# Work off PSUM traced in lagged steps, each placed behind its engine's instructions so far

## The chip, the cores and the metric

The kernel runs on one core of one Trainium2 chip. The metric is device microseconds of one execution; a time is the median of several runs. A core has a matrix engine (TensorE; PE in the profile, with its weight loads as PEld), VectorE (DVE), ScalarE (ACT), GpSimd (POOL) and DMA queues, most of which are fed here from the sync engine (SP). Each engine works off its own instructions in the order in which the program lists them, and waits at an instruction until the data and buffers that it needs are there.

## The reference

Eight batches of eight-head attention over 576 positions of width 64, with a causal mask, a bias of cumulated sums and a softmax; then a layer on the joined heads (512 channels): a two-dimensional Fourier transform of which the real part is kept, an addition, a normalisation, a two-layer net with a ReLU, and a residual.

```python
def _attn_ref(q, k, v, s):
    scores = scale * np.matmul(q, k.transpose(0, 1, 3, 2))        # (8, 8, 576, 576)
    cum = np.cumsum(np.maximum(s, 0.0), axis=-1)
    bias = -(cum[:, :, :, None] - cum[:, :, None, :])
    scores = np.where(causal, -1e9, scores + np.minimum(bias, 0.0))
    attn = np.exp(scores - np.max(scores, axis=-1, keepdims=True))
    attn = attn / (np.sum(attn, axis=-1, keepdims=True) + 1e-09)
    return np.matmul(attn, v)

def _moe_ref(x, w_ch1, w_ch2):                                    # x: (8, 576, 512)
    mixed = np.real(np.fft.fft(np.fft.fft(x, axis=1), axis=2))
    u = x + mixed
    un = (u - mean(u)) / np.sqrt(var(u) + 1e-06)                   # over the channels
    return u + np.maximum(un @ w_ch1, 0.0) @ w_ch2                 # 512 -> 2048 -> 512
```

## The kernel before, in words

To hold fp32 accuracy on TensorE, nearly every operand is split into a high part and the rest (`split`, L68 to L70: ACT copies the high part, DVE subtracts it), and a product is three passes: high by high, high by low, low by high.

**The attention loop.** 64 heads are worked in 32 pairs, `for i in range(NP)`, and an iteration holds pieces of several pairs: the score products whose row maxima are wanted for pair i+1 (`maxes`: a matmul into `pm`, L459, and a DVE reduction, L466; 12 of each), the high and low parts of the queries and keys (`high(i+2)`: ACT copies, L418 and L420; `low(i+1)`: the keys' rest `k` on DVE, L435, the queries' rest on POOL, L438), the scores and exponentials of pair i (`scores`: L491, L492 into `ps`, ACT's exponential L495), the product with the values of pair i-1 (`av`, into `pav`, moved out by ACT to `stage`, L527), and the division of pair i-2 (`recip` and `finish`: sums plus 1e-9 and a reciprocal on DVE, L538 and L539, out to memory and back as a broadcast `rb`, L544, then a product, L559, and its transfer into `xs`). `pm` and `pav` share five PSUM buffers; `ps` and the products of the Fourier stage share another pool of three.

Four pairs make a batch. When a batch is there, `folds` forms its symmetric and antisymmetric halves (`Aw`, `Bw`, `Df`, split into `De` and `Do`; L251 to L268) in iterations i with i % 4 == 2 (five of seven steps) and i % 4 == 3 (the rest), and `fourier` does the transforms in the iterations that follow: matmuls into `pzs` and `pzc`, split from PSUM into `zs` and `zc`, a second set into `pyc` and `pys`, sums `ym` and `yp` (L320, L321), and additions on POOL (L324 and on).

**The weights** come as 64-bit numbers in pieces of 256 columns, four for each of 16 blocks f of the net. `rounded` (L83 to L89) makes fp32 of one piece: exponent bits on DVE (L83), a scaled ReLU on ACT (L84), the mantissa on DVE (L85, L88), sign and exponent together on DVE (L87), a product on POOL (L89). In the attention loop `convert_w` writes the first blocks back to memory (L98). The remaining blocks are converted while the first token tile of the net runs (`load_w`): `rounded`, then the high part `wh` on ACT (L112) and the rest `wl`, on DVE for the first two pieces and on POOL for the last two (L114).

**The net** takes nine tiles of 512 tokens. Per block f: 12 matmuls into `h` (L183), which need the pieces 0 and 1 of `wh` and `wl`; `zh` on ACT (L187) and `zl` on DVE (L188); and 12 matmuls into four accumulators (L196 to L198), which need pieces 2 and 3.

**What sets the order.** TensorE's order is the order in which the program is traced (`manual_schedule`). The generators of an iteration are interleaved by `weave`, which at each turn advances the one that has used the smallest share of its own total; a `yield` returns a cost, and the second entry of each pair in the list is the total. The order of all other engines is made by a scheduler, from when an instruction was traced and from a model of when it could start; so an instruction there need not stand where it was traced.

## Time and profile before

| | |
|---|---|
| median of 3 runs | 1428.55 us (1426.3 to 1429.79) |
| the profiled execution's own time | 1426.1 us |
| its span in the profile | 1424.4 us |
| PE busy | 1305.1 us, 92% of the span, 6190 matmuls |
| DVE busy | 745.7 us, 52% |
| ACT busy | 539.3 us, 38% |
| POOL busy | 561.6 us, 39% |
| mean granted TensorE clock | 0.971 of full speed |

The page of the profile gives busy time by engine, the span in 40 slices of 35.6 us with the busy share of each in tenths, and groups of instructions by line. Other views give the engines' busy time in chosen windows, the waits with the instruction that ended each, and single instructions in order of time, with the idle time before one in brackets and what ended it. In a group's row the first number behind the bar is busy microseconds, the next mean nanoseconds of one, and behind the second bar stands the idle time ahead of them. The net's first tile starts some 600 us into the span, when the attention is done; from about 703 us on all weights are converted and eight tiles follow each other.

### The profile page before, as it was taken

How to read it: one execution, taken by the hardware profiler on the slowest of the kernel's cores; microseconds unless marked ns; L12 is line 12 of the kernel's file. 1: busy time of each engine (PE TensorE's matmuls, PEld its weight loads, DVE VectorE, ACT ScalarE, POOL GpSimd, SP SyncE). 2: the span in 40 equal slices, each digit the busy share in tenths (PEclk: the TensorE clock that was granted, in tenths of full speed). 3: DMA queues.
4: the chain of work that ended last, by engine and by line, in shares of the span. 5: the costliest groups of instructions: out<-in, count | busy, mean ns of one | idle time of the engine just before them, and what ended most of it. 6: DMA issues, size and time to landing. Idle time of an engine off the chain costs nothing.

```text
span 1424.4 us, 17997 instructions
## 1 busy us (share of the span) xinstructions
PE 1305.1 (92%) x6190; PEld 1068.7 (75%) x6190; DVE 745.7 (52%) x1684; ACT 539.3 (38%) x1211; POOL 561.6 (39%) x543
## 2 busy tenths in 40 slices
PE   4887979897988887997899999999999999999998
PEld 3766868686777676775688888888888888888886
DVE  6667677877777788799833233222332223322212
ACT  4775756676665656344321121211212112121110
POOL 6445465656546566565720402204022040123300
PEclk9998999999999997999899999999999999999999
DMA  8555556565655555433200000000000000000000
GB/s 214 156 159 144 163 149 180 158 168 159 159 161 144 166 149 163 162 123 121 79 8 30 31 30 15 15 30 31 30 15 15 30 30 30 15 16 0 30 0 30
DMA packets 78230, 125.05 MB, mean 88 GB/s; under 512 B 11256, under 2 KB 36249, under 8 KB 78139
## 3 DMA queue, kind: packets, MB, share of 16 engines
q1 hardware_dynamic: 75627, 119.83, 28.4%
q0 software_dynamic: 1696, 2.50, 0.9%
q10 hardware_dynamic: 816, 1.57, 0.3%
q8 instruction: 49, 0.80, 0.2%
q14 instruction: 42, 0.34, 0.1%
HBM read 76.85 MB, written 23.07 MB: 70 GB/s over the span
## 4 chain that ended last, share of the span: by engine, by line
PE 51%; DVE 7%; POOL 2%; DMA 1%; issue 1%; ACT 1%; SPq 0%; DVEq 0%; POOLq 0%; ACTq 0%
PE h L183 25%; PE acc L198 8%; PE acc L196 8%; PE acc L197 8%; POOL we L89 1%; DVE wm L88 1%; DVE we L83 1%; DVE wm L85 1%; DVE we L87 1%; DVE wl L114 1%; ACT wh L112 1%; DMA wl<-wD 0%; POOL wl L114 0%; DVE ucl L148 0%; DVE zl L188 0%
## 5 line engine op out<-in xcount | busy, mean ns | idle before, releaser
L188 DVE SCALAR_TENSOR_TENSOR zl<-h,zh 128x512 fp32r<-128x512 f32 x144 | 98.6, 686 | 405.5 <-ACT zh L187 405.4
L187 ACT ACTIVATE zh<-h 128x512 fp32r<-128x512 f32 x144 | 85.9, 596 | 530.1 <-PE h L183 530.1
L198 PE MATMUL acc<-zl,wh 128*128 128x512 f32 x576 | 227.5, 396 | 4.9 <-DVE zl L188 4.9
L196 PE MATMUL acc<-zh,wh 128*128 128x512 f32 x576 | 227.6, 395 | 1.0 <-ACT zh L187 1.0
L197 PE MATMUL acc<-zh,wl 128*128 128x512 f32 x576 | 226.8, 394 | 0.0
L523 PE MATMUL pavB<-P,va 128*128 128x320 f32 (+2 forms) x640 | 189.1, 389 | 9.5 <-ACT stage L527 8.9
L459 PE MATMUL pm<-KQ 128*128 128x256 f32 (+3 forms) x384 | 156.5, 427 | 44.4 <-DVE Mx L466 23.1
L495 ACT ACTIVATE P<-ps 128x320 f32<-128x320 f32 (+4 forms) x384 | 145.9, 393 | 110.5 <-PE ps L492 106.8
L491 PE MATMUL ps<-KQ 128*128 128x256 f32 (+2 forms) x384 | 154.1, 404 | 24.4 <-ACT P L495 14.0
L183 PE MATMUL h<-uch,wh 128*128 128x512 f32 x576 | 159.9, 398 | 8.3 <-ACT wh L112 8.3
L183 PE MATMUL h<-uch,wl 128*128 128x512 f32 x576 | 158.1, 396 | 0.8 <-DVE wl L114 0.8
L183 PE MATMUL h<-ucl,wh 128*128 128x512 f32 x576 | 156.9, 393 | 0.0
L466 DVE CUSTOM_DVE_ANT_0 trash<-pm,amask 128x128 bf16<-128x128 f32 (+3 forms) x256 | 123.5, 482 | 34.2 <-PE pm L459 16.9
L212 POOL TENSOR_TENSOR o<-o,w 128x512 f32<-128x512 f32 x32 | 41.8, 1305 | 252.3 <-issue 218.5
L183 PEld LDWEIGHTS h<-uch,wh 128*128 128x128 f32 x576 | 108.2, 190 | 35.9 <-ACT wh L112 12.1
L198 PEld LDWEIGHTS acc<-zl,wh 128*128 128x128 f32 x576 | 108.7, 189 | 32.0 <-DVE zl L188 6.9
L183 PEld LDWEIGHTS h<-uch,wl 128*128 128x128 f32 x576 | 109.2, 190 | 26.6 <-DVE wl L114 1.2
L196 PEld LDWEIGHTS acc<-zh,wh 128*128 128x128 f32 x576 | 108.6, 188 | 26.1 <-ACT zh L187 1.8
L183 PEld LDWEIGHTS h<-ucl,wh 128*128 128x128 f32 x576 | 108.9, 189 | 24.7
L197 PEld LDWEIGHTS acc<-zh,wl 128*128 128x128 f32 x576 | 108.6, 189 | 24.7
L459 PEld LDWEIGHTS pm<-KQ 128*128 128x128 f32 x384 | 78.4, 207 | 64.7 <-DVE Mx L466 30.2
L492 PE MATMUL ps<-q,k 128*128 128x256 f32 (+2 forms) x384 | 120.5, 316 | 3.1 <-POOL q L438 3.1
(140 smaller groups left out, 2066.9 us busy)
## 6 DMA issues: line engine op xcount, KB each, us to landing
qk<-in_qkT_dram SPq DMA_DIRECT2D x32, 576.0 KB
raw<-in_wP_dram SPq DMA_DIRECT2D x64, 256.0 KB
va<-in_vA_dram SPq DMA_DIRECT2D x32, 480.0 KB
q<-KQ SPq DMA_DIRECT2D x32, 288.0 KB
k<-KQ SPq DMA_DIRECT2D x32, 288.0 KB
rb<-rd SPq DMA_DIRECT2D x64, 144.0 KB
u<-uD SPq DMA_DIRECT2D x8, 1024.0 KB
out_dram<-o SPq DMA_DIRECT2D x32, 256.0 KB
```

The lines of the kernel that those rows point to most:

```text
L183: nc.tensor.matmul(h[:, :n], a[:, j * 128:(j + 1) * 128], b[:, j, :n], start=i == 0, stop=i == 11)
L187: nc.scalar.activation(zh[:, :n], h[:, :n], AF.Relu)
L188: nc.vector.scalar_tensor_tensor(out=zl[:, :n], in0=h[:, :n], scalar=0.0, in1=zh[:, :n].bitcast(F32), op0=ALU.max, op1=ALU.subtract)
L196: nc.tensor.matmul(acc[j][:, :n], a[:, cs], y[:, :n], start=g == 0, stop=False)
L197: nc.tensor.matmul(acc[j][:, :n], b[:, cs], y[:, :n], start=False, stop=False)
L198: nc.tensor.matmul(acc[j][:, :n], a[:, cs], z[:, :n], start=False, stop=g == NF - 1)
L459: nc.tensor.matmul(p[:, :n], qy[:, h, 128 * c:128 * c + 128], ky[:, h, k0:k0 + n], start=True, stop=True)
L466: nc.vector.tensor_tensor_reduce(out=trash[:nq, :n], in0=p[:nq, :n], in1=amask[:nq, m0:m0 + n], scale=1.0, scalar=first if x else NEG, op0 ...
L491: nc.tensor.matmul(p[:, :n], ky[:, h, ksl], qy[:, h, a:a + n], start=True, stop=False)
L492: nc.tensor.matmul(p[:, :n], k1[:, h, ksl], q1[:, h, a:a + n], start=False, stop=True)
L495: nc.scalar.activation(P[:, o:o + a + n - lo], p[:, lo - a:n], AF.Exp, scale=0.125)
L523: nc.tensor.matmul(p[:, a - lo:n], va[:, c, vs], P[:, o:o + w], start=c == 0, stop=c == cs[-1])
```

## The change

A new helper, `behind(engine)`, orders an instruction behind the last one that has been traced so far for that engine. It adds no wait on data. With it:

- `rounded` yields between its DVE, ACT and POOL steps. Its first and its last DVE operation, its ACT operation and its POOL product are each placed behind what their engines have so far; the mantissa pair stays free. The transfer in `convert_w` is placed behind SP's.
- `folds` makes each `Df`, its high part and its rest in three steps, the last two placed. Of a cost of 6.6 (7 before), 0.7 is worked off in iterations i % 4 == 2 and 0.3 in i % 4 == 3; before it was five sevenths and two sevenths.
- `fourier` places the rest of each split behind DVE's, half a step after the copy, and waits two more steps at its end before it writes out.
- The copies of `high`, the differences of `low` and the transfer of sums in `av` are placed. `low` and `high` start later in an iteration, and `low` at the same point in every iteration.
- `recip` and `finish` become one generator, `post`, in five steps, each placed.
- `weave` passes on the costs of what it interleaves, and `later` yields its delay in one piece.

```diff
+    def behind(engine):
+        return tc.issue_after(next(i for i in reversed(nc.cur_bb.bb.instructions) if i.engine == engine))
...
-        yield 0.0
+        yield 0.3
         e = pool.tile([128, WC], I32, tag="we", name="we", bufs=bufs)
-        nc.vector.tensor_scalar(e, hi, 0x7FF00000, None, op0=ALU.bitwise_and)
-        nc.scalar.activation(e, e, AF.Relu, bias=wbias, scale=8.0)
+        with behind(ET.DVE):
+            nc.vector.tensor_scalar(e, hi, 0x7FF00000, None, op0=ALU.bitwise_and)
+        yield 0.2
+        with behind(ET.Activation):
+            nc.scalar.activation(e, e, AF.Relu, bias=wbias, scale=8.0)
         nc.vector.tensor_scalar(m, hi, 0xFFFFF, 0x100000, op0=ALU.bitwise_and, op1=ALU.bitwise_or)
-        yield 0.4
-        nc.vector.scalar_tensor_tensor(out=e, in0=hi, scalar=-0x80000000, in1=e, ...)
         nc.vector.scalar_tensor_tensor(out=m.bitcast(F32), in0=lo, scalar=2.0 ** -16, in1=m, ...)
-        nc.gpsimd.tensor_mul(e.bitcast(F32), m.bitcast(F32), e.bitcast(F32))
-        yield 0.4
+        yield 0.2
+        with behind(ET.DVE):
+            nc.vector.scalar_tensor_tensor(out=e, in0=hi, scalar=-0x80000000, in1=e, ...)
+        yield 0.1
+        with behind(ET.Pool):
+            nc.gpsimd.tensor_mul(e.bitcast(F32), m.bitcast(F32), e.bitcast(F32))
+        yield 0.2
...
-            yield 1.0
-            d = fft.tile([128, 289], F32, tag="Df", name="Df")
-            nc.vector.tensor_add(d, a[:, 0:289], a[:, 576:287:-1])
-            split(De[0][:, jj], De[1][:, jj], d)
-            yield 1.0
...
+            yield 0.6
+            for D, n in ((De, 289), (Do, 288)):
+                d = fft.tile([128, 289], F32, tag="Df", name="Df")
...
+                yield 0.6
+                with behind(ET.Activation):
+                    nc.scalar.copy(D[0][:, jj], d[:, :n])
+                yield 0.6
+                with behind(ET.DVE):
+                    nc.vector.tensor_sub(D[1][:, jj], d[:, :n], D[0][:, jj].bitcast(F32))
+                yield 0.0
...
-            split(zs[0][:, c], zs[1][:, c], p[:96, 0:256])
-            yield 650
+            nc.scalar.copy(zs[0][:, c], p[:96, 0:256])
+            yield 325
+            with behind(ET.DVE):
+                nc.vector.tensor_sub(zs[1][:, c], p[:96, 0:256], zs[0][:, c].bitcast(F32))
+            yield 325
...
-            streams.append([later(low(i + 1), i % 4 == 0), (6, 7, 4, 3)[i % 4]])
+            streams.append([later(low(i + 1), 1.5), 7.5])
...
-            streams.append([high(i + 2), 6])
+            streams.append([later(high(i + 2), 2), 6.5])
...
-            streams.append([later(call(recip, i - 2), 4), 10])
-            streams.append([later(call(finish, i - 2), 6), 10])
+            streams.append([post(i - 2), 9.5])
...
-            streams.append([later(take(folding, 5), 2), 7 / 0.7])
+            streams.append([later(take(folding, FOLDS * 0.7), 1), 7])
...
-            streams.append([folding, FOLDS - 5])
+            streams.append([folding, FOLDS * 0.3])
...
-    recip(NP - 1)
-    finish(NP - 1)
+    weave([post(NP - 1), 1.0])
```

Three places show how the order moves. The first is DVE in an iteration with i % 4 == 2 (the fourth, i = 18), around the last reduction (`Mx_129`, L466 before and L498 in the changed file) of the iteration and the first of the next (`Mx_128`). Before, from the last reduction on:

```order
L256 TENSOR_TENSOR Df<-Aw 128x289
L321 TENSOR_TENSOR yp<-yc,pys 128x290
L435 TENSOR_TENSOR k_3723<-qk,KQ_121 64x576
L70 TENSOR_TENSOR De_3541<-Df,De_3540 128x289
L266 TENSOR_TENSOR eh<-e,eh 1x289
L260 TENSOR_TENSOR Df<-Bw 128x288
L435 TENSOR_TENSOR k_3723<-qk,KQ_121 64x576
L70 TENSOR_TENSOR Do_3543<-Df,Do_3542 128x288
L466 ISA trash,Mx_128<-pm,amask 128x128
```

Now, at the same place:

```order
L270 TENSOR_TENSOR Df<-Aw 128x289
L281 COPY e<-xs 1x1
L498 ISA trash,Mx_128<-pm,amask 128x128
L498 ISA Mx_128 128x1
L278 TENSOR_TENSOR De_3523<-Df,De_3522 128x289
L272 TENSOR_TENSOR Df<-Bw 128x288
L98 SCALAR_TENSOR_TENSOR we<-raw,we 128x256
L498 ISA trash,Mx_128<-pm,amask 128x256
```

The two operations on the keys (`k`, 64x576) stood ahead of the next iteration's first reduction and now stand in the middle of its reductions; the second `De` and `Df<-Bw` now stand behind the first of them, the second `Do` and the `eh` behind the last. Between the last reduction of the one iteration and the first of the next there are 16 operations before and 13 now; three of the 13 belong to `rounded` (L90, L94 and L95).

The second place is DVE in the first tile of the net, one block of weights (f = 11: pieces we_7263, we_7275, we_7287). Before:

```order
1276 L83 TENSOR_SCALAR we_7275<-raw_7273 128x256
1277 L85 TENSOR_SCALAR wm_7272<-raw_7273 128x256
1278 L88 SCALAR_TENSOR_TENSOR wm_7272<-raw_7273,wm_7272 128x256
1279 L87 SCALAR_TENSOR_TENSOR we_7275<-raw_7273,we_7275 128x256
1280 L114 TENSOR_TENSOR wl11_7230<-we_7263,wh11_7229 128x256
1281 L83 TENSOR_SCALAR we_7287<-raw_7285 128x256
```

Now (L90 is the L83 of before, L94 the L85, L95 the L88, L98 the L87, L126 the L114):

```order
1308 L126 TENSOR_TENSOR wl11_7230<-we_7263,wh11_7229 128x256
1309 L90 TENSOR_SCALAR we_7275<-raw_7273 128x256
1310 L94 TENSOR_SCALAR wm_7284<-raw_7285 128x256
1311 L95 SCALAR_TENSOR_TENSOR wm_7284<-raw_7285,wm_7284 128x256
1312 L98 SCALAR_TENSOR_TENSOR we_7275<-raw_7273,we_7275 128x256
1313 L94 TENSOR_SCALAR wm_7296<-raw_7297 128x256
1314 L95 SCALAR_TENSOR_TENSOR wm_7296<-raw_7297,wm_7296 128x256
1315 L126 TENSOR_TENSOR wl11_7230<-we_7275,wh11_7229 128x256
1316 L90 TENSOR_SCALAR we_7287<-raw_7285 128x256
```

The first operation of a piece (L83, now L90) stood ahead of the `wl` of the piece before it and now stands behind it, for each of the pieces 1 and 2; the mantissa pair runs a piece ahead.

The third place is DVE where attention ends, with the last pair's sums (`sums_6291`) and its product (`xr_6502`). Before:

```order
1122 L538 TENSOR_SCALAR sums_6291<-sums_6291 32x36
1123 L539 RECIPROCAL sums_6291<-sums_6291 32x36
...
1132 L320 TENSOR_TENSOR ym_6454<-yc_6442,pys_6444 128x290
...
1136 L321 TENSOR_TENSOR yp_6485<-yc_6472,pys_6474 128x290
1137 L559 TENSOR_TENSOR xr_6502<-stage_6290,rb_6499 128x576
```

Now:

```order
1160 L346 TENSOR_TENSOR ym_6454<-yc_6442,pys_6444 128x290
...
1163 L347 TENSOR_TENSOR yp_6485<-yc_6472,pys_6474 128x290
1164 L578 TENSOR_SCALAR sums_6291<-sums_6291 32x36
1165 L579 RECIPROCAL sums_6291<-sums_6291 32x36
...
1168 L594 TENSOR_TENSOR xr_6502<-stage_6290,rb_6499 128x576
```

The sums and their reciprocal stood ahead of the last `ym` and `yp` and now stand directly behind them.

More of the change, by code (lines that the diff above doesn't have):

```diff
@@ L97, in convert_w @@
                 m = yield from rounded(pool, f, x, bufs)
-                nc.sync.dma_start(out=wD[f, :, WC * x:WC * x + WC], in_=m)
-                yield 0.2
+                with behind(ET.SP):
+                    nc.sync.dma_start(out=wD[f, :, WC * x:WC * x + WC], in_=m)
     def load_w(pool, f):
@@ L294, in fourier @@
             nc.tensor.matmul(p[:n, 0:258], eh[:, t0:t0 + n], cor, start=False, stop=True)
-            split(zc[0][:n, c], zc[1][:n, c], p[:n, 0:258])
-            yield 870
+            nc.scalar.copy(zc[0][:n, c], p[:n, 0:258])
+            yield 435
+            with behind(ET.DVE):
+                nc.vector.tensor_sub(zc[1][:n, c], p[:n, 0:258], zc[0][:n, c].bitcast(F32))
+            yield 435
         for x in range(2):
@@ L325, in fourier @@
             nc.gpsimd.tensor_add(xs[:, kc, 289:576], xs[:, kc, 289:576], ym[:, 287:0:-1])
+        yield 300
+        yield 300
         ts = slice(b * S, (b + 1) * S)
@@ L417, in high @@
         for h in range(2):
-            nc.scalar.copy(ky[64:128, h], qk[64:128, h])
+            with behind(ET.Activation):
+                nc.scalar.copy(ky[64:128, h], qk[64:128, h])
             yield 1.0
-            nc.scalar.copy(qy[64:128, h, 0:S], qk[0:64, h])
+            with behind(ET.Activation):
+                nc.scalar.copy(qy[64:128, h, 0:S], qk[0:64, h])
             yield 1.0
@@ L434, in low @@
         for h in range(2):
-            nc.vector.tensor_sub(k1[0:64, h], qk[64:128, h], ky[64:128, h].bitcast(F32))
+            with behind(ET.DVE):
+                nc.vector.tensor_sub(k1[0:64, h], qk[64:128, h], ky[64:128, h].bitcast(F32))
             yield 1.0
         for h in range(2):
-            nc.gpsimd.tensor_sub(q1[64:128, h], qk[0:64, h], q1[0:64, h].bitcast(F32))
+            with behind(ET.Pool):
+                nc.gpsimd.tensor_sub(q1[64:128, h], qk[0:64, h], q1[0:64, h].bitcast(F32))
             yield 1.0
@@ L530, in av, with post @@
                     yield 4 * w / 2.4
-            nc.sync.dma_start(out=sums[16 * h:16 * h + 16], in_=r1 if h else x[64:65])
+            if h:
+                yield 100
+            with behind(ET.SP):
+                nc.sync.dma_start(out=sums[16 * h:16 * h + 16], in_=r1 if h else x[64:65])
         st.update(x=x, sums=sums)
-    def recip(i):
-        st = sts[i]
-        sums = st["sums"]
-        nc.vector.tensor_scalar_add(sums, sums, 1e-9)
+    xbuf = {}
+    def post(i):
+        st = sts.pop(i)
+        sums, x, b, j = st["sums"], st["x"], st["b"], st["j"]
+        yield 3.0
+        with behind(ET.DVE):
+            nc.vector.tensor_scalar_add(sums, sums, 1e-9)
         nc.vector.reciprocal(sums, sums)
+        yield 0.5
         rd = dram.tile([32, 36], F32, tag="rd", name="rd", bufs=4)
-        nc.sync.dma_start(out=rd, in_=sums)
+        with behind(ET.SP):
+            nc.sync.dma_start(out=rd, in_=sums)
+        yield 1.5
         rb = attb.tile([128, S], F32, tag="rb", name="rb", bufs=2)
-        for h in range(2):
-            nc.sync.dma_start(out=rb[64 * h:64 * h + 64], in_=rd[16 * h:16 * h + 16].rearrange("a f -> (a f)").partition_broadcast(64))
-        st["rb"] = rb
-    xbuf = {}
-    def finish(i):
-        st = sts.pop(i)
-        b, j, rb = st["b"], st["j"], st["rb"]
+        with behind(ET.SP):
+            for h in range(2):
+                nc.sync.dma_start(out=rb[64 * h:64 * h + 64], in_=rd[16 * h:16 * h + 16].rearrange("a f -> (a f)").partition_broadcast(64))
+        yield 2.0
         if j == 0:
@@ L696, in later @@
 def later(gen, n):
-    for _ in range(n):
-        yield 1.0
+    yield n
     yield from gen
@@ L712, in mixed @@
         try:
-            s[2] += next(s[0])
+            c = next(s[0])
         except StopIteration:
@@ L716, in mixed @@
         else:
-            yield 1.0
+            s[2] += c
+            yield c
 def _tables():
```

33 lines of the change are left out of this document (18 added, 15 removed).

## The prediction

> **What bounds the kernel now.** I read the page's totals and slices first, then the engines' busy time by stage, then the waits of the stage that has any, and last the single instructions around the longest. The page:
>
> ```profile
> span 1424.4 us, 17997 instructions
> PE   4887979897988887997899999999999999999998
> PEclk9998999999999997999899999999999999999999
> ```
>
> ```profile
> 50.00:555.00 505.00, 435.68 (x2451) 366.99 (x2449) 373.91 (x1048) 322.88 (x803) 288.42 (x296) 0.95 0.57 159
> 630.00:690.00 60.00, 49.44 (x188) 36.18 (x187) 56.78 (x131) 28.55 (x64) 34.28 (x42) 0.94 0.34 114
> 690.00:703.00 13.00, 9.76 (x31) 7.15 (x30) 10.83 (x12) 4.86 (x9) 10.61 (x9) 0.76 0.24 81
> 703.00:1424.00 721.00, 715.77 (x3101) 582.00 (x3099) 207.92 (x272) 125.73 (x213) 154.30 (x114) 1.00 0.06 22
> ```
>
> The second fence is the view of busy time by window: bounds, length, then PE, PEld, DVE, ACT, POOL with their counts, granted clock, DMA share, GB/s. Behind 703 us PE is busy 715.77 of 721 us at full clock: the eight later tiles are bound by TensorE and the change does not reach them. There 3101 matmuls take 721 us, so one of the net takes 0.2325 us and the 24 of a block 5.6 us. What can move lies ahead. In the attention loop (50 to 555 us) PE is idle for 505 − 436 = 69 us and runs at 0.95 of its clock, though DVE has 26% to spare on the average. In the first tile of the net (630 to 690 us) DVE is full, 56.78 of 60 us, and POOL is not: there the conversion of the weights sets the pace. The waits of PE in the loop, with total, number and longest:
>
> ```profile
> PE pm L459 <- DVE Mx L466: 22.4, 11, 5.5
> ...
> PE ps L491 <- ACT P L495: 14.0, 17, 2.2
> ...
> PE pavB L523 <- ACT stage L527: 8.9, 13, 1.6
> ...
> PE pm L459 <- ACT stage L527: 2.4, 4, 0.7
> ```
>
> The first is few and long. Three of its eleven, from the instructions in order of time:
>
> ```profile
> 196.87 0.69 PE L459 MATMUL pm<-KQ 128*128 128x384 f32 x1 [4.30 <-DVE Mx L466]
> ...
> 330.14 0.69 PE L459 MATMUL pm<-KQ 128*128 128x384 f32 x1 [5.45 <-DVE Mx L466]
> ...
> 397.68 0.44 PE L459 MATMUL pm<-KQ 128*128 128x384 f32 x1 [2.87 <-DVE Mx L466]
> ```
>
> They come 67 us apart (133 over the first gap), that is once in four pairs: where a batch's folds meet the two `k` operations of `low`. What DVE does between the reduction of 317.43 and that of 329.80; the first six us of it are folds too and left out:
>
> ```profile
> 317.43 0.53 DVE L466 CUSTOM_DVE_ANT_0 trash<-pm,amask,M 64x320 bf16<-64x320 f32 x1
> ...
> 323.88 1.49 DVE L435 TENSOR_TENSOR k<-qk,KQ 64x576 fp32r<-64x576 f32 x1
> 325.41 0.94 DVE L70 TENSOR_TENSOR De<-Df,De 128x289 fp32r<-128x289 f32 x1
> 326.38 0.93 DVE L266 TENSOR_TENSOR eh<-e,eh 1x289 fp32r<-1x289 f32 x1
> 327.35 0.77 DVE L260 TENSOR_TENSOR Df<-Bw 128x288 f32<-128x288 f32 x1
> 328.15 1.24 DVE L435 TENSOR_TENSOR k<-qk,KQ 64x576 fp32r<-64x576 f32 x1
> 329.42 0.46 DVE L70 TENSOR_TENSOR Do<-Df,Do 128x288 fp32r<-128x288 f32 x1
> 329.80 0.28 DVE L466 CUSTOM_DVE_ANT_0 trash<-pm,amask 128x128 bf16<-128x128 f32 x1
> ```
>
> The reduction of 329.80 empties the `pm` buffer that the matmul of 330.14 wants; it needs nothing of the six operations ahead of it, it only stands behind them. The stall costs more than itself:
>
> ```profile
> 325.00:330.00 5.00, 0.00 (x0) 0.00 (x0) 4.84 (x7) 1.19 (x3) 5.00 (x6) 0.83 0.08 28
> 330.00:335.00 5.00, 4.02 (x10) 2.85 (x10) 3.67 (x13) 2.72 (x7) 2.63 (x3) 0.50 0.87 280
> ```
>
> After 5.45 us without work the clock is 0.50 for the next 5 us, about 2.5 us lost.
>
> **The change, part by part.** The sum is made against the profiled execution (1426.1 us, 1.7 beyond its span); the median of the runs is 2.4 above it, and I add that at the end.
>
> *A1, the long DVE stalls.* By the new order the two `k` (1.49 + 1.24), the second `De` (0.94), the `eh` (0.93), the second `Df<-Bw` (0.77) and the last `Do` (0.46) leave the stretch ahead of the first reduction: 5.8 us. Three operations of `rounded` come in, at 0.28 to 0.44 us each, about 1.0. The stretch shrinks by 4.8, from 11.9 us (317.9 to 329.8) to about 7; that is close to the stall itself, and the other long stalls are shorter than this one. Of 22.4 us I take 16 away. The bounds are 0 (the `k` pair, now amid the reductions, holds those up as long) and 22.4.
>
> *A2, the waits on ACT.* Three rows above, 14.0 + 8.9 + 2.4 = 25.3 us, where an exponential or a `stage` copy stands behind other ACT work. The copies of `high` and of the folds are now spread, each behind what ACT has, rather than in groups. No row says how many of the 34 waits have such a copy ahead; I take a third, 8. The bounds are 0 and 25.
>
> *A3, the clock.* 5% of 435.68 us of busy time, some 22 us, is the price of the throttled clock in this stage, at 2.5 us a long stall and less for short ones. If two thirds of the long stalls and a third of the short ones go, some quarter of it, 6 us, comes back. The bounds are 0 and 22.
>
> *B, the conversion of the weights in the first tile.* Rows of the groups by line, 630 to 690 us: count, busy us, mean ns of one, idle time ahead.
>
> ```profile
> L87 DVE SCALAR_TENSOR_TENSOR we<-raw,we 128x256 int32<-128x256 int32 x27 | 15.6, 581 | 0.2
> L84 ACT ACTIVATE we<-we,wbias 128x256 int32<-128x256 int32 x26 | 13.0, 508 | 9.0 <-DVE we L83 8.7
> L83 DVE TENSOR_SCALAR we<-raw 128x256 int32<-128x256 int32 x26 | 11.5, 441 | 0.0
> L112 ACT CAST wh<-we 128x256 fp32r<-128x256 f32 x28 | 11.4, 406 | 21.9 <-POOL we L89 21.8
> L114 POOL TENSOR_TENSOR wl<-we,wh 128x256 fp32r<-128x256 f32 x13 | 11.3, 870 | 6.2 <-ACT wh L112 6.2
> L114 DVE TENSOR_TENSOR wl<-we,wh 128x256 fp32r<-128x256 f32 x14 | 6.7, 479 | 1.9 <-ACT wh L112 1.8
> L187 ACT ACTIVATE zh<-h 128x512 fp32r<-128x512 f32 x7 | 4.1, 584 | 0.0
> L89 POOL TENSOR_TENSOR we<-wm,we 128x256 f32<-128x256 f32 x29 | 25.9, 897 | 21.1 <-DVE we L87 19.1 <-DVE wm L88 2.1
> ```
>
> 27 L87 in 60 us are 2.22 us a piece, 8.9 us a block of four. This speaks against the change. In the new order the first operation of pieces 1 and 2 stands behind the `wl` of the piece before, and L87 behind its own first operation, so what used to overlap becomes one chain: product, `wh`, `wl`, first operation, ACT's ReLU, L87, next product. Around a block: four products (4 × 0.897), four `wh` (4 × 0.406), two `wl` on POOL (2 × 0.870), two on DVE (2 × 0.479), and for pieces 1 and 2 L83, L84 and L87 (2 × (0.441 + 0.508 + 0.581)), in all 11.0 us. That is 2.1 us a block more. Ten blocks are converted in this tile; I charge eight of them, since ahead of 630 us the end of the attention shares DVE and sets the pace: +17. Against it: in the 13 us from 690 on PE, at clock 0.76, still waits for the normalisation of the next tile; in a longer first tile that work is done in the chain's idle time, and half of the 13, 6 us, is regained. So +11. The bounds are 0 (the waits fall where DVE would have stood still anyway) and +37 (below, the slower case).
>
> *C, the end of attention.* The last pair's sums now go behind the last `yp`.
>
> ```profile
> 562.17 0.17 DVE L538 TENSOR_SCALAR sums<-sums 32x36 f32<-32x36 f32 x1 [0.82 <-DMA sums<-rows]
> ...
> 573.96 0.46 DVE L321 TENSOR_TENSOR yp<-yc,pys 128x290 f32<-128x290 f32 x1 [0.76 <-POOL xs L324]
> 577.46 0.76 DVE L559 TENSOR_TENSOR xr<-stage,rb 128x576 f32<-128x576 f32 x1 [3.05 <-DMA rb<-rd]
> 581.51 0.76 DVE L251 TENSOR_TENSOR Aw<-xa,xs 128x576 f32<-128x576 f32 x1 [2.09 <-DMA xs<-xr]
> ```
>
> ```profile
> SPq L544 <- DMA rd<-sums: 11.9, 13, 2.6
> ```
>
> `yp` ends at 574.4; sums and reciprocal take 0.6, the way out to `rd` up to 2.6, the broadcast 3.1, the product 0.76 and its way into `xs` with the rest up to `Aw` 3.3: `Aw` starts at 584.8 instead of 581.5, +4 rounded up. Queued behind on DVE are the folds of the last batch and so its whole transform; the first tile runs meanwhile, so 0 is the lower bound, and 8, both DMA legs doubled, the upper.
>
> *D, the rest.* SP's transfers, POOL's `q` and the steps of `fourier` move by parts of an iteration; the spread of the last over two more steps costs no instruction, and its cover is PE's work of the same iteration (435.68 of 505 us). I put them at 0, with bounds of −8 and +8, about one of the groups of waits either way.
>
> Sum: −16 − 8 − 6 + 11 + 4 = −15 on 1426.1, 1411; beside the median, 1413.5, say 1414 us.
>
> **The rivals.**
>
> *Larger gain, about 1400.* B costs nothing. For it: POOL is the scarce partner in the chain, and DVE's operations already stand still beside POOL's, so that putting them later moves waits, not work:
>
> ```profile
> 649.54 0.85 POOL L89 TENSOR_TENSOR we<-wm,we 128x256 f32<-128x256 f32 x1 [1.02 <-DVE we L87]
> 649.72 0.82 DVE L83 TENSOR_SCALAR we<-raw 128x256 int32<-128x256 int32 x1
> 651.79 0.28 DVE L83 TENSOR_SCALAR we<-raw 128x256 int32<-128x256 int32 x1
> ```
>
> The same L83 takes 0.82 us beside POOL's product and 0.28 alone. A first operation that now waits for `wl` can come out at 0.28 instead of 0.441, and the whole chain then loses up to 0.3 us a piece, 1.3 a block with L87's share: 9.7, near the 8.9 of now. 1428.5 − 30 + 4 = about 1402, or 1394 if A2 is twice what I took; I say 1400, with 1388 to 1405 around it. Against it: the chain still has one wait more a piece. [...]
>
> *Little change, about 1429.* The folds' work is the same and DVE is full around it (4.84 of 5 us above), so the burst only moves: the reductions of the middle wait for the `k` pair instead of those of the start. Then A1 to A3 give half, −15, and B and C take 15: 0. Against it: five `pm` buffers stand ahead of a reduction in mid-iteration, and the `k` pair has only 2.7 us.
>
> *Slower, about 1439: TensorE falls to half its clock beside the conversion chain.* One mechanism: with a round of 11.0 us and 5.6 us of matmuls, PE is idle 5.4 us a block, as long as the stall at 330 that brought 0.50. At half clock the 12 matmuls of `h` take 5.6 us, not 2.8, and `zh` (0.584) stands on ACT ahead of the last piece's `wh`. From the second `wl` to there the other branch, L83, L84, L87, product, `wh`, `wl` and product, takes 0.441 + 0.508 + 0.581 + 0.897 + 0.406 + 0.870 + 0.897 = 4.6; `h` and `zh` take 6.2, and the round becomes 11.0 + 1.6 = 12.6. That is 3.7 us a block over 8.9, in all ten blocks, since TensorE and not DVE is then the slow partner ahead of 630 us too: +37, and nothing regained behind 690 us, where the next tile starts at half clock. With A and C as above, 37 + 4 − 30 = +11 on 1428.5. It decides from a round of some 10.5 us on, where the matmuls' pause reaches 5 us. [...] For it: the clock is already 0.94 in 630 to 690 and 0.76 behind. Against: the matmuls come in several groups a round, so no pause need last 5 us.
>
> *That the change does not do what it says:* where the scheduler's order was the traced one already, nothing moves; the three places shown rule this out for the terms that count. I give it no chance of its own.
>
> **How the numbers follow.** The forecast 0.40 (own range 1403 to 1424), the larger gain 0.20, little change 0.15, slower 0.25. This kernel's runs span 3.5 us, so that about 0.3%, 4.3 us, can be told from no change. Faster by more than that: the forecast and the larger gain, 0.60. Within: little change, 0.15. Slower: 0.25. The range, 1388 to 1442, takes in the larger gain and the slower case with a few us beyond; it leaves out their far ends (A in full with B and C at nothing, 1359; B at +37 with A at a third, 1460).
>
> **What would show it.** A1: no wait of PE on `Mx` over 2 us, their total under 8 us, and the clock in the loop at 0.97. A2: the waits on P and `stage` together under 20 us. B: `zl` of the first tile 11 us apart, the idle time of ACT's `wh` under POOL's product longer than 21.8 us, DVE well under 56 of 60 us. C: the last `Aw` 10 us behind the last `yp`. The prediction is wrong if the `zl` stay 9 us apart or less (then B is no cost and 1400 is near), if they come to over 12 with the clock near half (then 1439), or if PE's idle time between 50 and 555 us stays at 69 us.

## The result, and the profile after

The changed kernel takes 1462.32 us (median of 4 runs, 1460.43 to 1465.72) against 1427.47 us before: a ratio of 1.0245, 95% interval 1.0221 to 1.0269. It is 35 us slower, and lies above the forecast range of 1388 to 1442. On a second chip the ratio was 1.0206 (1.0189 to 1.0224). The profiled execution has a time of 1462.36 us and a span of 1460.6. Some executions ran at a lower granted clock and far longer (the profiled one of x1 below took 1516 us at 0.835); they are left out, so x1 has no stretches in the tables. The page after:

```profile
span 1460.6 us, 17994 instructions
...
PE   4987988887897966876699999999999999999998
...
PEclk9999999999999987989999999999999999999999
```

Over the first fourteen slices (499 us before, 511 now) PE's digits have the same sum as before, 109; in the next six they are 6, 6, 8, 7, 6, 6 where before stood 8, 7, 9, 9, 7, 8. The same in windows (PE, PEld, DVE, ACT, POOL, clock):

```profile
50.00:505.00 455.00, 394.92 (x2257) 332.17 (x2257) 347.75 (x974) 301.70 (x742) 247.74 (x265) 0.97 0.58 160
555.00:640.00 85.00, 69.06 (x327) 58.15 (x328) 52.65 (x109) 27.31 (x61) 33.56 (x34) 0.85 0.29 97
640.00:700.00 60.00, 42.34 (x163) 30.27 (x161) 41.28 (x101) 21.48 (x48) 27.77 (x36) 0.97 0.32 111
```

In the tile DVE, which was full (56.78 of 60 us from 630 to 690), is now 41.28 of 60 busy: none of the engines is full there, they wait for each other. To place the loss I read five landmarks, the starts of four operations and the end of the span, off the instructions in order of time, in every kernel's profile: the transpose of the maxima of pair 30 on PE (pairs counted from 0; the expectations call it the 30th), the last `yp` of batch 6, the first `Aw` of batch 7 (the expectations and the prediction call it the last `Aw`), the last `yp` of batch 7, and the end of the span. All in us:

| kernel | transpose of pair 30 at | to the last yp of batch 6 | to Aw of batch 7 | to the last yp | to the end |
|---|---|---|---|---|---|
| before | 509.6 | 64.4 | 7.5 | 41.2 | 801.7 |
| changed | 502.0 | 78.9 | 13.8 | 46.0 | 819.9 |
| difference | -7.6 | +14.5 | +6.3 | +4.8 | +18.2 |

The sum is +36.2, the difference of the spans. The loop gained little; every stretch behind it lost. The four losses have different places:

**The last iteration (+14.5) and the last transform (+4.8).** PE's long waits there, from the instructions in order of time:

```profile
536.03 0.79 PE L135 MATMUL mu<-th,ones 128*128 128x512 f32 x1 [6.08 <-ACT P L527]
...
555.30 0.53 PE L304 MATMUL pzs<-dsin,Do 128*96 128x256 f32 x1 [11.49 <-DVE Do L278]
...
629.71 1.59 PE L304 MATMUL pzs<-dsin,Do 128*96 128x256 f32 x6 [6.60 <-DVE zc L321]
```

The second is the longest stall of the program behind its start. Its `Do` on DVE:

```profile
526.20 0.87 DVE L272 TENSOR_TENSOR Df<-Bw 128x288 f32<-128x288 f32 x1
...
554.80 0.45 DVE L278 TENSOR_TENSOR Do<-Df,Do 128x288 fp32r<-128x288 f32 x1
```

`Df` is there at 527.1, `Do` is made at 554.8. Between the two DVE waited 4.31 us for the tile's input and then worked off the normalisation and the conversion, which had been traced ahead of `Do`. Before the change the same `Do` came at 535.4, ahead of nearly all of that work:

```profile
535.44 1.04 DVE L70 TENSOR_TENSOR Do<-Df,Do 128x288 fp32r<-128x288 f32 x1
```

**The last sums (+6.3).**

```profile
580.83 0.46 DVE L347 TENSOR_TENSOR yp<-yc,pys 128x290 f32<-128x290 f32 x1 [0.52 <-POOL xs L350]
...
581.63 0.37 DVE L579 RECIPROCAL sums<-sums 32x36 f32<-32x36 f32 x1
...
590.59 0.76 DVE L594 TENSOR_TENSOR xr<-stage,rb 128x576 f32<-128x576 f32 x1 [4.06 <-DMA rb<-rd]
...
594.66 0.76 DVE L263 TENSOR_TENSOR Aw<-xa,xs 128x576 f32<-128x576 f32 x1 [2.68 <-DMA xs<-xr]
```

**The first tile (+18.2).** One piece of weights to the next, across POOL, ACT and DVE:

```profile
656.86 0.72 POOL L101 TENSOR_TENSOR we<-wm,we 128x256 f32<-128x256 f32 x1
657.61 0.40 ACT L124 CAST wh<-we 128x256 fp32r<-128x256 f32 x1 [1.52 <-POOL we L101]
658.05 0.42 DVE L126 TENSOR_TENSOR wl<-we,wh 128x256 fp32r<-128x256 f32 x1 [1.73 <-ACT wh L124]
...
658.39 0.29 DVE L90 TENSOR_SCALAR we<-raw 128x256 int32<-128x256 int32 x1
...
658.77 0.51 ACT L93 ACTIVATE we<-we,wbias 128x256 int32<-128x256 int32 x1 [0.76 <-DVE we L90]
...
659.32 0.42 DVE L98 SCALAR_TENSOR_TENSOR we<-raw,we 128x256 int32<-128x256 int32 x1
...
659.82 0.73 POOL L101 TENSOR_TENSOR we<-wm,we 128x256 f32<-128x256 f32 x1 [2.24 <-DVE we L98]
```

Each starts as the one before it ends: 2.96 us from product to product, and POOL waits 2.24 of them. The `zl` of two blocks of this tile:

```profile
686.82 0.68 DVE L200 SCALAR_TENSOR_TENSOR zl<-h,zh 128x512 fp32r<-128x512 f32 x1
697.37 0.68 DVE L200 SCALAR_TENSOR_TENSOR zl<-h,zh 128x512 fp32r<-128x512 f32 x1
```

They come 10.55 us apart. Two neighbours of before:

```profile
669.52 0.68 DVE L188 SCALAR_TENSOR_TENSOR zl<-h,zh 128x512 fp32r<-128x512 f32 x1
678.14 0.68 DVE L188 SCALAR_TENSOR_TENSOR zl<-h,zh 128x512 fp32r<-128x512 f32 x1
```

From the last `yp` to the last `zl` of the tile it takes 97.0 us (640.7 to 737.7), 74.2 before: +22.8. Five blocks at this pace (from the ninth `zl` to the fourteenth) take 52.1 us in place of 40.0, +12.1. The last two take 30.7 in place of 18.7, since the next tile's normalisation now stands among their conversion. That is only moved: the next tile's first `zl` comes 1.0 us behind the last one of this tile, 12.3 before, −11.3. So at the next tile's first `zl` the loss is +11.5. The rest behind that is +6.7: 11 matmuls of the first tile are still to be done there (2.6 us), PE waits 1.8 us for the output `o` (L216), and the clock is 0.66 from 747 to 752 us.

In the loop, the waits of PE from 50 to 555 us:

```profile
PE pmt L503 <- DVE Mx L498: 18.8, 16, 2.5
PE pm L491 <- DVE Mx L498: 13.5, 11, 3.8
PE ps L523 <- DMA KQ<-mt: 9.2, 7, 3.2
PE mu L135 <- ACT P L527: 6.1, 1, 6.1
PE pavA L555 <- DVE Mx L498: 5.6, 8, 2.2
...
PE ps L523 <- ACT P L527: 2.5, 3, 1.1
PE pm L491 <- ACT stage L559: 1.5, 7, 0.2
```

The waits on ACT's P and `stage` fell from 25.3 to 4.0 us; the 6.1 us of `mu` are not in this, since they fall into the last iteration, shown above. Those on the reductions rose from 24.3 us (22.4 at `pm`, 1.0 at `pmt`, 0.9 at `pavA` and `pavB`) to 37.9, half of them at a new place: the transpose `pmt`, which needs the last reduction of a pair. All in all PE is idle 60.1 us from 50 to 505, 63.7 before.

### The profile page after: what moved, and what is told of

It reads as the page before. It is cut to its first block, busy times and chain, and to the rows that moved or that the text cites. A ratio compares the mean times of both kernels' runs of the same rounds, so it can differ in the third digit from the quotient of the medians.

```text
span 1460.6 us, 17994 instructions
## 1 busy us (share of the span) xinstructions
PE 1307.4 (90%) x6190; PEld 1066.1 (73%) x6190; DVE 749.7 (51%) x1684; ACT 542.1 (37%) x1211; POOL 544.5 (37%) x543
## 4 chain that ended last, share of the span: by engine, by line
PE 49%; DVE 5%; POOL 2%; ACT 1%; DMA 1%; issue 1%; SPq 0%; ACTq 0%; DVEq 0%; POOLq 0%
PE h L195 24%; PE acc L208 8%; PE acc L210 8%; PE acc L209 8%; POOL we L101 1%; DVE we L98 1%; DVE we L90 1%; DVE wl L126 1%; ACT we L93 1%; ACT wh L124 1%; DVE wm L95 1%; DMA raw<-in_wP_dram 0%; DVE wm L94 0%; POOL wl L126 0%; PE pyc L332 0%
## 5 line engine op out<-in xcount | busy, mean ns | idle before, releaser
L498 DVE CUSTOM_DVE_ANT_0 trash<-pm,amask 128x128 bf16<-128x128 f32 (+3 forms) x256 | 124.4, 486 | 79.3 <-PE pm L491 67.2
L224 POOL TENSOR_TENSOR o<-o,w 128x512 f32<-128x512 f32 x32 | 41.3, 1292 | 249.4 <-issue 215.4
L470 POOL TENSOR_TENSOR q<-qk,q 64x576 fp32r<-64x576 f32 x64 | 98.4, 1556 | 63.3 <-DMA q<-KQ 44.8
```

Of the source, the lines that this page charges most:

```text
L470: nc.gpsimd.tensor_sub(q1[64:128, h], qk[0:64, h], q1[0:64, h].bitcast(F32))
L498: nc.vector.tensor_tensor_reduce(out=trash[:nq, :n], in0=p[:nq, :n], in1=amask[:nq, m0:m0 + n], scale=1.0, scalar=first if x else NEG, op0 ...
```

## The experiments

Each is compared with the kernel before on its own chip. The table carries on the one above; the rows of one kernel come from one profiled execution.

| kernel | ratio (95%) | pair 30 at | to yp | to Aw | to yp | to the end |
|---|---|---|---|---|---|---|
| y4, changed again | 1.0206 (1.0189 to 1.0224) | 504.4 | 77.4 | 14.0 | 45.1 | 819.3 |
| x1, tile by the old rounded | 1.0077 (1.0055 to 1.0099) | | | | | |
| x2, folds of batch 6 free | 1.0192 (1.0149 to 1.0235) | 507.8 | 76.6 | 14.0 | 45.2 | 818.9 |
| x3, last two divisions as before | 1.0203 (1.0164 to 1.0242) | 505.1 | 78.0 | 7.6 | 48.3 | 821.2 |
| t1, first operation free | 1.0178 (1.0128 to 1.0227) | 506.5 | 76.8 | 13.6 | 45.2 | 815.3 |
| t2, before + first operation placed | 1.0090 (1.0065 to 1.0115) | 513.0 | 66.7 | 7.7 | 41.2 | 816.2 |
| y2, nothing placed | 1.0175 (1.0160 to 1.0191) | 534.4 | 68.2 | 7.6 | 41.3 | 802.2 |
| w_folds, only the folds placed | 1.0135 (1.0107 to 1.0163) | 529.9 | 68.1 | 8.2 | 42.0 | 802.0 |
| v1, only high placed | 1.0127 (1.0077 to 1.0177) | 530.8 | 67.7 | 7.6 | 41.5 | 801.2 |
| v2, all but high placed | 1.0296 (1.0234 to 1.0358) | 518.8 | 76.1 | 13.8 | 46.0 | 818.9 |
| x4, low and high as before | 1.0345 (1.0299 to 1.0392) | 528.7 | 77.9 | 14.6 | 45.8 | 819.9 |
| z3, low as before | 1.0220 (1.0192 to 1.0249) | 507.3 | 78.5 | 13.8 | 44.9 | 821.0 |
| z4, k on POOL | 1.0228 (1.0200 to 1.0256) | 502.7 | 79.2 | 13.7 | 44.8 | 818.7 |
| y3, low later | 1.0483 (1.0465 to 1.0501) | 541.8 | 77.5 | 14.0 | 45.7 | 819.0 |
| z2, nothing placed from the last iteration on | 0.9972 (0.9952 to 0.9992) | 502.9 | 69.1 | 8.7 | 42.6 | 803.0 |
| z2 again, other chip | 0.9996 (0.9976 to 1.0015) | 511.1 | 69.4 | 8.3 | 40.8 | 803.7 |

For y4 1.0245 within 0.003 was expected; 1.0206 is just outside. One kernel more, y1, frees the end by other means (the old `rounded` in the tile, no placing in the folds and splits of batches 6 and 7, the last two divisions as before); it does not compute what the reference does, so nothing is read from its time.

The stretches of a row come from one execution, and in the loop two executions of one kernel lie up to 8 us apart (z2, the last two rows). So smaller differences in the column of pair 30 tell nothing.

### The tile: x1, t1, t2

x1 takes the whole of the old `rounded` back for the tile.

```diff
-            m = ... (yield from rounded(stage, f, x, nstage))
+            m = ... (yield from rounded_free(stage, f, x, nstage))   # the body before the change
```

> The changed kernel, but in the first tile of the net the weights are converted by the old rounded (no placing, the old yields); everything else as changed. In the changed kernel zl of the first tile come 10.6 us apart (8.4 before) and the stretch from the last yp to the end is 18 us longer than before. Theory (the chain of placed operations sets the pace there): zl about 8.5 us apart again, 1462 - 18 = about 1444 us. Rival (the pace is set by what else changed, the later end of the attention and the lower clock beside the idle PE): zl stay over 10 us apart, 1460 to 1464.

A ratio of 1.0077, where the changed kernel has 1.0206 to 1.0245: 18 to 24 us less, the theory; the pace of 8.5 us that it named has no profile to show it. What in `rounded` does it, t1 and t2 ask. t1 frees one of the four placed operations; t2 places this one alone in the kernel before.

```diff
-        with behind(ET.DVE):
-            nc.vector.tensor_scalar(e, hi, 0x7FF00000, None, op0=ALU.bitwise_and)
+        nc.vector.tensor_scalar(e, hi, 0x7FF00000, None, op0=ALU.bitwise_and)
```

> The changed kernel, but in the first tile of the net the first operation of a piece (the exponent bits, L90) is not placed; the other three placed operations of rounded are. It then stands ahead of the wl of the piece before, and only the last DVE operation stands behind it. Theory (the prediction's chain: the first operation and ACT's ReLU behind wl, 0.44 + 0.51 us for two pieces of a block): 10.6 - 1.9 = 8.7 us from zl to zl, the stretch from the last yp to the end at 805 us, ratio 1.008 to 1.012. Rival (placing the last operation or POOL's product suffices to make the chain): zl over 10 us apart, ratio 1.018 or more.

> The kernel before with one thing of the change: in the first tile the first operation of a piece is placed behind what DVE has so far, and so stands behind the wl of the piece before. Nothing else is changed. Theory: zl 10 to 10.6 us apart (8.4 before), the stretch from the last yp to the end 12 to 18 us longer, ratio 1.008 to 1.013. Rival (it takes the other placings too, or the late end of the attention): within 3 us of before.

In t2 two `zl` of the tile:

```profile
684.28 0.68 DVE L215 SCALAR_TENSOR_TENSOR zl<-h,zh 128x512 fp32r<-128x512 f32 x1
694.15 0.69 DVE L215 SCALAR_TENSOR_TENSOR zl<-h,zh 128x512 fp32r<-128x512 f32 x1
```

This pair, 9.87 us apart, is the slowest of three alike (9.7 to 9.9); on the mean of the tile it is 9.0, 7.9 before. Expected were 10 to 10.6. The stretch to the end is 14.5 us longer and the time 0.9%, both as the theory had them. This one placement, and with it the order "`wl` of a piece, then the first operation of the next", makes 14.5 us by itself, where the whole change has 18.2. Taken out of the changed kernel it does not give as much back. In t1:

```profile
682.18 0.68 DVE L225 SCALAR_TENSOR_TENSOR zl<-h,zh 128x512 fp32r<-128x512 f32 x1
691.16 0.68 DVE L225 SCALAR_TENSOR_TENSOR zl<-h,zh 128x512 fp32r<-128x512 f32 x1
```

```profile
730.39 0.79 PE L160 MATMUL var<-th,ones 128*128 128x512 f32 x1 [5.58 <-ACT th L75]
```

The pace is the 8.98 us that the chain without L90 and L93 predicts (8.7), and the last `zl` of the tile comes 78.9 us behind the last `yp`, not 97.0. But the first of the next tile comes 97.7 us behind it (98.0 in the changed kernel): now the normalisation of that tile is late, as PE's wait for `var` shows, and of the 18 us only 4.6 are left at the end of the span. Expected were 805 us, measured 815.3: the pace was right, the gain was not. Why the normalisation comes that late in t1 stays open.

### The end of the attention: x2, x3

x2 takes the placing out of the folds of batch 6 (the three-step form stays); x3 divides the last two pairs as before the change.

```diff
-            folding = folds(b, *xbuf[b])
+            folding = (folds_free if b >= 6 else folds)(b, *xbuf[b])   # x2: no behind() in it
```

```diff
-    weave([post(NP - 1), 1.0])
+    recip(NP - 1)                                                      # x3, and the same for NP - 2
+    finish(NP - 1)
```

> The changed kernel, but the folds of the last batch but one (the one whose second step falls into the last iteration) are traced in the same lagged steps without being placed behind their engines. In the changed kernel the second Do of that batch stands behind 25 operations of the normalisation and the conversion on DVE and PE waits 11.5 us for it. Theory (that wait is a loss of its own on the path): the wait goes, Do at about 535 us, 1462 - 10 = about 1452 us. Rival (the last sums, not Do, set when the last batch is folded; PE's wait only moves): 1459 to 1464, the last Aw still at about 594 us.

> The changed kernel, but the division of the last two pairs (sums, reciprocal, broadcast, product) is traced as before the change, at once and not placed. On DVE the last sums then stand ahead of the last ym and yp again. Theory (the sums behind the last yp lengthen the way to the last batch's folds by 13.9 - 7.5 = 6.4 us and the rest of the program hangs on it): last Aw some 6 us after where it would be else, that is at 588 us, 1462 - 6 = about 1456 us. Rival (the last batch's transform is hidden behind the first tile): 1460 to 1464.

In x2 `Do` is made at 532.5 and PE's wait of 11.5 us is gone. The longest wait behind the loop is now

```profile
PE pzc L346 <- DVE zs L340: 8.7, 1, 8.7
```

that is, for the rest of the first Fourier split, which is placed as well and stands behind the same work. The stretch is 76.6 us instead of 77 to 79: the rival, with one wait in place of another. In x3 `Aw` comes 7.6 us behind `yp` (13.8 in the changed kernel, 7.5 before), which is the theory; 2 to 3 of the 6.3 us are lost again in the next stretch (48.3), and the time of 1461.8 us is the rival's. x2 loses what it frees to the next placed operation on the same queue; where x3 loses it is not known. That suggests freeing them all, which is z2 below.

### What the placing does, and where: y2, z2

```diff
     def behind(engine):
-        return tc.issue_after(...)
+        return ExitStack() if not placing[0] else tc.issue_after(...)
...
         streams = []
+        placing[0] = i < NP - 1      # z2; y2 has no behind() at all
```

> The changed kernel with every step traced where it is, but none placed behind its engine: the finer steps, the new delays and totals alone. Theory (placing costs at the end of the attention and in the tile and is worth little in the loop): about the time before, ratio 0.995 to 1.005. Rival (placing is what spreads ACT's and DVE's work in the loop; without it the steps pile up again, and the finer steps have bursts of up to 22 operations between two batches of reductions where before had 17): ratio 1.01 or more, waits of PE on the maxima above 30 us.

> The changed kernel, but nothing is placed any more from the last iteration of the loop on (steps, delays and totals as changed). Without any placing the stretches behind the loop were as long as before the change (7.6 us from the last yp of batch 6 to the last Aw, 41.3 to the last yp, 802.2 to the end), and the placed loop was 5 to 8 us ahead of the old one at its 30th transpose. Theory (placing costs only from the last iteration on): both together, ratio to before 0.997. Rival (the placed loop hands over a state in which the rest is late anyway, as where the end was freed by other means): ratio 1.004 or more.

In y2 the rival holds. Without any placing three of the four stretches behind the loop are as before the change (7.6, 41.3, 802.2) and the first is 3.8 us longer (68.2), but pair 30 comes at 534.4 us, 25 us later than before and 30 later than with the placing. The waits of its loop (50 to 505 us):

```profile
PE pm L477 <- DVE Mx L484: 34.2, 17, 7.9
PE ps L509 <- ACT P L513: 12.4, 13, 2.2
PE ps L509 <- DMA KQ<-mt: 7.4, 8, 2.1
```

So the finer steps with their new delays and totals make the loop worse, and placing repairs it; behind the loop placing makes nearly all of the loss. z2 places in the loop and not from the last iteration on, and is about the sum of the good stretches (69.1, 8.7, 42.6 and 803.0 behind the loop, each 1 to 5 us longer than before): 0.9972 (0.9952 to 0.9992) where 0.997 was expected. On another chip, as the measure for v1, it came out at 0.9996 (0.9976 to 1.0015), outside the 0.002 around 0.997 that were expected. It beats the changed kernel by over 2%; against the kernel before it is equal or a few us faster.

> The changed kernel, nothing placed from the last iteration of the loop on, once more, as the measure for the kernel with only high placed on the same chip: ratio 0.997 within 0.002.

### The loop: x4, z3, z4, y3

These ask what the 18.8 us at the transposes are worth. x4 takes back `low` and `high`, z3 `low` alone, y3 starts `low` later, z4 computes the keys' rest on POOL:

```diff
-            with behind(ET.DVE):
-                nc.vector.tensor_sub(k1[0:64, h], ...)
+            with behind(ET.Pool):
+                nc.gpsimd.tensor_sub(k1[0:64, h], ...)                 # z4
```

> The changed kernel, but high and low are traced as before the change: not placed, at their old delays and totals. In the changed kernel PE waits 18.8 us in 16 places for the last reductions ahead of the transpose of the maxima (pmt), where the two k operations now stand amid the reductions; before it had 22.4 us in 11 places at the first reductions. Theory (the k operations carry the stall wherever they stand): the waits at pmt fall under 6 us, those at pm rise to 20 us, and the time stays within 4 us of 1462. Rival (the later place of k and of high is what made the loop 7.6 us shorter by its 30th transpose): the loop gives those back, 1468 to 1472.

> The changed kernel, but low alone as before (old delays and totals, not placed); high, with ACT's copies, as changed. With low and high both old the waits at the transposes were gone (2.8 us), but those on ACT's exponentials came to 28.8 us and the loop was 25 us longer. Theory (the k operations amid the reductions cost the waits at the transposes, the later high is what freed ACT; they are separate): waits at pmt under 6 us, on P under 8 us, 30th transpose at 495 us or sooner, ratio 1.012 to 1.016. Rival (k where it was stands in the folds' bursts again, 16 operations between reductions): waits at pm of 20 us or more, 30th transpose at 505 to 530 us, ratio 1.02 to 1.04.

> The changed kernel with the keys' rest (k) computed on POOL in place of DVE, at the same place in the program. It takes 64 operations of 1.1 to 1.5 us away from DVE amid the reductions. Theory (k on DVE makes the last reductions late): waits of PE on the maxima (pm, pmt, pav together 38 us) fall below 20 us; POOL goes from 57% to some 70% of the loop; ratio 1.01 to 1.015. Rival (the folds, not k, hold up the reductions, and POOL's queue then makes q and k late): the waits on the maxima stay above 28 us or waits on POOL take their place, ratio 1.02 or more.

> The changed kernel with low starting later in its iteration (delay 5 of 11 in place of 1.5 of 7.5), so that the k operations come nearer the end of the reductions. Theory (the two k operations amid the reductions make the last ones late and carry the 18.8 us of waits at the transpose): these fall under 10 us and the time falls by some 5 us against the changed kernel on the same chip. Rival (whatever stands there holds up a reduction: the waits go back to the first reductions, and the queries' rest on POOL, now later too, adds waits of its own at the scores): no change or slower, ps waits on POOL over 8 us.

z4 is the clearest. Its waits (50 to 505 us):

```profile
PE ps L523 <- DMA KQ<-mt: 15.4, 8, 3.7
PE pm L491 <- DVE Mx L498: 8.4, 6, 3.5
PE pm L491 <- DMA KQ<-cumD: 8.3, 4, 3.4
PE ps L523 <- ACT P L527: 6.9, 5, 2.4
```

The waits on the reductions fell from 35.8 to 12.8 us (8.4, 3.5 at `pav`, 0.9 at the transposes; both up to 505 us), as the theory had it, and the loop is no shorter: 502.7 us, among the 502 to 511 of the kernels with the changed loop. The transfer of the maxima, the table rows and the exponentials make 31 us of waits in their place (14 in the changed kernel), so PE's idle time falls by 7.6 us only, from 60.1 to 52.5. Its busy time rises by as much, from 394.9 to 402.6 for ten matmuls more, at a clock of 0.94 instead of 0.97. The ratio of 1.0228 is the rival's, but waits on POOL did not come (3.8 us, 5.5 in the changed kernel). z3 moves `k` back: the waits return to the first reductions (22.2 us) and P (10.2), 507.3 us, the rival. y3, with `low` later, is 40 us slower in the loop (up to 505 us 35.8 us of waits at `pm` and 17.9 on the maxima's transfer). x4 missed both its theory and its rival (1482 us). Its waits on P are 28.8 us and its loop is 25 us longer; `low` alone (z3) does not do this, so it is `high`, whose copies come early again.

### Which placing carries the loop: w_folds, v1, v2

> The changed kernel with only the folds' copies and rests placed; rounded, the Fourier splits, high, low, the sums and the division are traced in the same steps but not placed. Without any placing the loop's 30th transpose came at 534 us (502 to 504 with all of it), with 34.2 us of waits at the first reductions. Theory (the placing of the folds is what spreads the bursts): 30th transpose at 510 us or sooner, waits at pm under 20 us; behind the loop as without placing, but for the wait on the last Do; ratio 1.00 to 1.01. Rival (it is the placing of high and low, or all of it together): 30th transpose at 525 us or later, ratio 1.012 or more.

> The changed kernel with only the ACT copies of high placed, everything else in the new steps but not placed. The copies stand where the scheduler puts them without placing, some twenty ACT instructions earlier, in the kernel before too. Theory (placing the copies of high is what the loop's gain consists of; placing the folds alone gave nothing): 30th transpose at 510 us or sooner (534 without any placing, 530 with the folds placed), waits of PE on P and stage under 6 us together, and behind the loop the stretches of the kernel without placing; ratio 0.995 to 1.003. Rival (it takes all of the placing together): 30th transpose at 522 us or later, ratio 1.01 or more.

> The changed kernel with everything placed but the copies of high. Theory (as above): the loop loses what it gained, 30th transpose at 522 us or later, waits on P and stage over 18 us, ratio 1.035 or more. Rival (the other placings carry the gain): 30th transpose at 502 to 508 us, ratio 1.02.

In each only the `with behind(...)` lines named are kept or left out. Folds alone give 4.5 of the 30 us and `high` alone 3.6, no more than the scatter; all but `high` give 15.6. The theories of w_folds and v1 fell and their rivals hold: neither of the two placings carries the loop alone. v2, at 518.8 us and 1.0296, lies between its theory and its rival. It takes `high` and others together. That PE's next wait, on the other engine, is always close behind would explain it, and is not shown.

## Why the prediction was wrong

The forecast was -15 on the profiled execution, and it became +36. The error of 51 us divides into 22 in A, 19 in D, 7 in B and 2 in C. Two steps failed: the price of the removed waits (A), and D, put at nothing. The sign that the text itself named came too: from 50 to 555 us PE is idle 80.7 us (17 of them in the two long waits of the last iteration), not less than 69.

**A1 failed** at "Of 22.4 us I take 16 away". The long waits at the first reduction fell from 22.4 to 13.5 us, but the wait moved to the last reduction: 37.9 us in all instead of 24.3. This is the lower bound that the text named (the `k` pair holds up the reductions it now stands amid), and the mechanism of the rival "little change"; z3 and z4, without the `k` pair there, have 0.5 and 0.9 us left at the transposes. The deeper error is in the price. A stall was priced at its own length and its clock, as if PE ran on to the end of the loop without it. z4 took 23 us of such waits away and gained nothing.

**A2 was undersized**: 21 us of the waits on ACT went, not 8. **A3** was right in direction: clock 0.97 instead of 0.95 up to 505 us. Together A was to give 30 us; up to pair 30 it gave 7.6 in this execution. Seven executions with the same loop show 502 to 511 us, on their mean 4 us less than the one profile of before, and 7 less than t2, which has the loop of before (513.0).

**B was right in its mechanism**, and its sum too small. The chain was forecast at 11.0 us a block and is 10.6; t2 shows that its one cause makes most of the loss. Charged were 2.1 us in eight blocks less 6 regained, +11, and at the next tile's first `zl` it is +11.5. That they agree is in part luck: five blocks cost 2.4 us each, and the wait for the next tile's normalisation was not regained but moved into the last two blocks. The +6.7 behind it were not in the sum. +18.2 in place of +11.

**C** was +4 and is +6.3. The legs `rd`, `rb` and `xs` were right to half a microsecond (2.7, 3.6 and 3.3 us for 2.6, 3.1 and 3.3); `Aw` came 13.4 us behind the end of `yp`, not 10.4, because from the reciprocal (582.0) to the product (590.6) it takes 8.6 us, and the sum had 5.7 (2.6 and 3.1). Most of the difference is a queue again: the transfer into `rd` is placed behind SP's, and SP issues it at 584.3 us, 2.3 behind the reciprocal, since three transfers of the batch before (`uD`) stand ahead of it and one of them waits for POOL until 583.1.

**D was put at nothing and cost 19.3 us**, well beyond its bounds of 8. The reason given was that the steps of `fourier` cost no instruction and PE's work of the same iteration covers them; the placed folds of the last iteration had no term at all. In the loop no such loss shows. In the last iteration the cover is gone: DVE's queue holds the normalisation and the first tile's conversion, and a placed operation stands behind all of it. The stretch up to the last `yp` of batch 6 is 14.5 us longer and the last transform 4.8. Of the 14.5 up to 5 do not belong to the placing, for they are still there in y2 and z2 (68.2 and 69.1 us against 64.4; t2, with the old steps, has 66.7). For C the prediction asked what is queued ahead at the place where the program changes, for D it did not; it could have been read from the new order of DVE in the last iteration.

**The rivals.** The slower case was priced at 1439 by a half clock in every round, which did not come: at a round of 10.6 us the clock is 0.97 from 640 to 700 us. From 664 to 706 it is 1.00, though PE is busy only 27 of these 42 us. Nor did the half clock need a pause of 5 us, which the rival took from one stall of 5.45. The one spell near half clock in this stretch (0.57 on the mean of 659 to 663) stands behind a pause of 2.34 us. Before the change there were three from 676 to 704 us: 0.57 from 676 to 680 behind pauses of 1.40 and 0.36 us, 0.59 from 686 to 690 behind 0.87 and 1.70, and 0.50 from 698 to 703 behind 0.57 and 2.67. In the changed kernel's rounds from 664 to 706, at clock 1.00, the longest pause is 1.74 us, and one of 2.17 ahead of 708.2 is followed by 1.00 too (708 to 712). As far as these rows tell, the rival failed by little. The length of one pause does not tell the spells from the rest, and what does is not shown.

The larger gain rested on two rows of one operation, L83 at 0.82 us beside POOL's product and at 0.28 alone. In the piece shown above L90 takes 0.29 us behind `wl`; on the mean of all pieces from 640 to 700 us it takes 0.42, 0.44 before. That DVE stands still beside POOL was the author's estimate from those two rows. The product took 0.916 us on the mean where DVE was busy 56.80 of the 60 us, and takes 0.763 where it is busy 41.28. Before and after, 640 to 700 us:

```profile
L89 POOL TENSOR_TENSOR we<-wm,we 128x256 f32<-128x256 f32 x23 | 21.0, 916 | 17.9 <-DVE we L87 15.8 <-DVE wm L88 2.1
```

```profile
L101 POOL TENSOR_TENSOR we<-wm,we 128x256 f32<-128x256 f32 x21 | 16.0, 763 | 27.0 <-DVE we L98 27.0
```

The 0.13 us a product below the 0.897 of the sum, 0.5 us a block, explains the 10.6 in place of 11.0, and no more: POOL's idle time ahead of the product rose from 17.9 to 27.0.

**Still open**: what sets the loop's pace once the waits on DVE and on ACT are gone. The waits that then appear, on the maxima's transfer and the table rows, and the lower clock are read from z4, not tested by a kernel that removes them.

## What to carry to other kernels

In this kernel, tying an operation behind all that its engine has so far helped within a steady loop (pair 30 at 502.0 us, 534.4 in y2) and was expensive where the program changes stage (958.6 us from there to the end, 919.3 in y2); ask for the last iteration by itself, and for each engine and the DMA queue, what has been traced ahead. Where engines hand work to and fro, moving one operation from ahead of another's result to behind it can join overlapping pieces to one chain; the rows of the groups gave its price well here (11.0 us for 10.6). A removed wait need not be worth its length, as z4 shows (23 us of waits gone, pair 30 at 502.7 us instead of 502.0): price it by what the consumer would wait for next, and where no row tells, take a small share of it.

## What the runs showed that was not expected

Two executions of one kernel (z2) on two chips had pair 30 at 502.9 and 511.1 us, and their spans differ by 7.0 us (1426.3 and 1433.3): in this kernel nearly all of the scatter arises in the attention loop, and the stretches behind it repeat within 2 us. A difference of a few us in the loop of a single profile says nothing here. And finer steps with new delays and totals, with no instruction more and no placing, cost 25 us of a 510 us loop (y2).
